# A spectral filter and feed-forward kernel: mirrored filter rows gathered in 7 of 16 blocks, after another piece of the input

## The chip, the cores and the metric

The kernel runs on one core of one Trainium2 chip. The metric is device time in microseconds (us) of one execution. A core has five engines that run at once, each through its own queue of instructions in order: TensorE (PE: matmuls, with its weight loads shown as PEld), VectorE (DVE), ScalarE (ACT), GpSimd (POOL) and SyncE (SP, which here only issues transfers). Transfers (DMA) are issued from the queues of SP, ACT and POOL and run beside the engines. An engine waits for another, or for a transfer, on a semaphore.

## The reference

One input x of 2048 rows and 448 columns goes through two kinds of layer, each twice. The first is a filter in the frequency domain, the second a feed-forward block with a squared relu; each is fed by a layer norm and added to x.

```python
def _A_ref(x, w_r, w_i):                     # x: [1, 2048, 448], w: [2048, 225]
    X = jnp.fft.rfft2(x.astype(jnp.float32), axes=(-2, -1))
    X = X * (w_r + 1j * w_i)
    return jnp.fft.irfft2(X, s=(S, D), axes=(-2, -1)).astype(jnp.bfloat16)

def _B_ref(x, w1, b1, w2, b2):               # 448 -> 1792 -> 448
    h = jnp.einsum("bsd,df->bsf", x, w1) + b1
    r = jnp.where(h > 0, h, 0)
    return jnp.einsum("bsf,fd->bsd", r * r, w2) + b2

x = A_x
x = x + _A_ref(_layernorm(x), A_w_r, A_w_i)
x = x + _B_ref(_layernorm(x), B_w1, B_b1, B_w2, B_b2)
x = x + _A_ref(_layernorm(x), A_w_r, A_w_i)
x = x + _B_ref(_layernorm(x), B_w1, B_b1, B_w2, B_b2)
```

All data are bfloat16, sums are float32.

## The kernel before

The 2048 rows are 16 row tiles of 128 (row 16p + t of x is partition p of tile t). All of x stays on the chip. The transforms are matmuls with constant matrices, in stages:

- *Norm and first transform* (tags A1, `ln_stats`, `first_A`). For each tile VectorE takes mean and variance (BN_STATS, BN_AGGR, lines 790 and 791), or ACT does with two passes over the tile (line 778); ACT takes a square root (line 654), VectorE the reciprocal (line 797). The transform matrix FA, scaled by that reciprocal, is Fs (line 672, GpSimd or VectorE); minus twice the mean is m (line 802). TensorE multiplies the tile with Fs, and ACT brings the sums from PSUM to XA (line 660). `GROUPS1` says which tiles are normed together and which of them on ACT (second number 1).
- *First filter* (`spectral(True)`): a transform along the columns (TD), one along the rows (B), the products with W (`stage_W`, tag W0) and the way back (Bi). The frequencies of the rows are in pairs p = 0 to 7. B's results for a pair are two halves, E and F. The products run on VectorE alone (TENSOR_TENSOR, line 687), first for pair 1, then 2 and 3, 4 and 5, 6 and 7, and last 0; each result Z is what Bi's matmuls wait for.
- *Feed-forward* (TI, AI, ln, h, o), a second norm and first transform (A2), the second filter (TD1 to Bi1) and the second feed-forward block.

W has to be there in rows as they come and in mirrored rows, since a pair uses a frequency and its mirror. `Wt` holds four slots for each pair 1 to 7: w_r, mirrored w_i, w_i, mirrored w_r. The two straight ones are plain loads on SP's queue. For the mirrored ones the kernel gathers: an iota makes a list of partitions in reverse (`back`, line 733), two gathers on GpSimd's queue (line 703) read w_i and then w_r by that list into `Wm`, which lies in the memory of yT, and 14 GpSimd copies (line 661, tags M.0 to M.6) take from each gathered row of 16 blocks of 225 the block that a pair needs, its columns 1 to 224. Pair p needs block 16 - p; the copies are blocks 15 down to 9.

The gathers are tied to one more thing than their list: the last argument of `gather` is a piece of x, `xin[:, 8, :]`, so that they start only when the piece with tile 8 has arrived.

The order of work on each engine is not that of the code. Every piece of work is a unit with a tag, and the table `ORDER` gives each unit a rank; `schedule` sorts by rank, hands out PSUM banks, and puts small filler matmuls (line 1302) where its own clock says that TensorE would be idle. A letter behind a rank puts the unit on ACT (a), VectorE (d) or GpSimd (p).

## Time and profile before

| | us |
|---|---|
| median of 3 runs | 276.46 |
| lowest and highest of them | 275.58, 277.64 |
| the profiled execution's own time | 275.05 |
| its span, from first to last instruction | 273.3 |
| busy in it: TensorE, VectorE, ACT, GpSimd | 259.6, 217.0, 169.5, 15.1 |

The profile is one execution. A line of its timeline has the start and length in us, the engine, the line of the kernel, the operation, what it writes and reads with their shapes, how many alike were merged, and in brackets how long the engine was idle before and what ended that. `<-issue` means that no wait shows. TensorE is busy for 95% of the span. The chain that ended last is followed back from the last instruction: at each step to what released it, or to the instruction before it on its engine.

### The profile page before, as it was taken

The page shows a single profiled execution, that of the slowest core. Times are in us where ns is not written, and L with a number is a line of the kernel's source. Part 1 is how long each engine was busy: PE and PEld are TensorE (multiplying, and loading weights), DVE is VectorE, ACT ScalarE, POOL GpSimd, SP SyncE. Part 2 cuts the span into 40 slices and gives each one's busy share as a digit, 9 for nine tenths or more (in the row PEclk, how much of TensorE's full clock was granted, in tenths as well). Part 3 has the DMA queues.
Part 4 walks back from the last instruction along what each step waited for, and adds up shares of the span by engine and source line. Part 5 has one row for each costly group of instructions (what it writes and reads, how often), then busy time and mean ns, then how long its engine had stood idle before and what let it go on. Part 6 is the DMA issues. An engine that isn't in the chain of part 4 may idle for free.

```text
span 273.3 us, 5853 instructions
## 1 busy us (share of the span) xinstructions
PE 259.6 (95%) x2198; PEld 158.6 (58%) x2198; DVE 217.0 (79%) x678; ACT 169.5 (62%) x387; POOL 15.1 (6%) x41
## 2 busy tenths in 40 slices
PE   8599749999999999999999999999999999999996
PEld 2477425779754554455557875779754454454554
DVE  5764899699999888697999999799697776345932
ACT  5796728698624982788314898597815834888000
POOL 2550800000000000000000000000000000000000
PEclk9999989999999999999999999999999999999999
DMA  6999590002220233100000000002130024200114
GB/s 192 375 323 305 172 306 23 0 2 40 41 44 25 43 52 59 38 2 0 2 1 0 5 2 0 0 5 41 38 70 6 0 58 93 57 2 0 36 46 139
DMA packets 27584, 18.06 MB, mean 66 GB/s; under 512 B 20226, under 2 KB 26082, under 8 KB 27428
## 3 DMA queue, kind: packets, MB, share of 16 engines
q1 hardware_dynamic: 26548, 14.87, 20.4%
q0 software_dynamic: 288, 1.84, 2.3%
q10 hardware_dynamic: 720, 0.98, 1.1%
q8 instruction: 17, 0.28, 0.5%
q14 instruction: 11, 0.09, 0.1%
HBM read 12.18 MB, written 1.84 MB: 51 GB/s over the span
## 4 chain that ended last, share of the span: by engine, by line
PE 81%; DVE 9%; DMA 6%; issue 1%; POOL 1%; ACTq 0%; ACT 0%; DVEq 0%
PE ps L635 81%; DVE tmp L687 5%; DMA yT<-in_A_w_r_dram,back 4%; DMA xin<-in_A_x_dram 2%; DVE x_sb L1078 2%; DVE arena L687 1%; DVE tmp L661 1%; DVE st L790 0%; POOL Fs L672 0%; ACTq L627 0%; DVE Fs L672 0%; ACT L727 0%; DVE x_sb L687 0%; POOL Wt L661 0%; DVE x_sb L1198 0%
## 5 line engine op out<-in xcount | busy, mean ns | idle before, releaser
L635 PE MATMUL ps<-yT,W_sb 64*128 64x512 bf16 (+1 forms) x770 | 89.8, 346 | 0.0
L635 PE MATMUL ps<-W_sb,arena 128*128 128x448 bf16 (+2 forms) x490 | 87.3, 336 | 0.0
L635 PEld LDWEIGHTS ps<-yT,W_sb 64*128 64x128 bf16 (+1 forms) x770 | 51.1, 95 | 36.4 <-issue 1.3
L635 PEld LDWEIGHTS ps<-W_sb,arena 128*128 128x128 bf16 x490 | 46.2, 98 | 36.7 <-DVE arena L1128 0.4
L654 ACT ACTIVATE arena<-ps,b1col 128x512 bf16<-128x512 f32 x84 | 51.8, 691 | 19.1 <-PE ps L635 19.0
L687 DVE TENSOR_TENSOR arena<-arena 128x512 bf16<-128x512 bf16 (+1 forms) x140 | 44.8, 363 | 17.0 <-ACT arena L654 16.9
L660 ACT ACTIVATE arena<-ps 128x448 bf16<-128x448 f32 (+1 forms) x41 | 24.3, 698 | 11.3 <-PE ps L635 11.1
L1102 ACT ACTIVATE VT<-x_sb 128x448 bf16<-128x448 bf16 x32 | 18.4, 577 | 19.9 <-DVE x_sb L1078 19.9
L1198 DVE SCALAR_TENSOR_TENSOR x_sb<-ps,arena 128x448 bf16<-128x448 f32 (+2 forms) x27 | 15.1, 564 | 9.6 <-PE ps L635 9.5
L654 ACT ACTIVATE mv<-mv,epst 128x1 f32<-128x1 f32 (+1 forms) x45 | 12.5, 297 | 13.0 <-DVE mv L791 6.8
L660 ACT ACTIVATE XA<-ps 128x512 bf16<-128x512 f32 x32 | 17.1, 593 | 4.7 <-PE ps L635 4.7
L654 ACT ACTIVATE arena<-ps 128x256 bf16<-128x256 f32 x56 | 17.1, 393 | 3.3 <-PE ps L635 3.2
L660 ACT ACTIVATE VT<-ps 128x512 bf16<-128x512 f32 (+1 forms) x27 | 13.9, 618 | 4.9 <-PE ps L635 4.9
L687 DVE TENSOR_TENSOR tmp<-arena,Wt 128x896 bf16<-128x896 bf16 (+1 forms) x24 | 12.3, 554 | 4.7 <-POOL Wt L661 4.6
L635 PE MATMUL ps<-yT,VT 64*128 64x512 bf16 x42 | 15.8, 376 | 0.0
L635 PE MATMUL ps<-arena,G_sb 128*128 128x448 bf16 (+1 forms) x76 | 15.3, 347 | 0.1
L635 PE MATMUL ps<-HS_sb,arena 128*128 128x512 bf16 x64 | 14.7, 379 | 0.1
L635 PE MATMUL ps<-H_sb,arena 128*128 128x256 bf16 x64 | 9.4, 292 | 5.5 <-DVE arena L687 5.4
L635 PE MATMUL ps<-TD_sb,XA 112*64 112x112 bf16 (+2 forms) x312 | 13.1, 224 | 0.0
L635 PEld LDWEIGHTS ps<-TD_sb,XA 112*64 112x64 bf16 (+2 forms) x312 | 12.1, 108 | 1.2 <-ACT arena L660 0.4
L635 PE MATMUL ps<-Fs,xin 128*128 128x256 bf16 x64 | 9.1, 272 | 3.5 <-POOL back L733 3.4
L635 PEld LDWEIGHTS ps<-H_sb,arena 128*128 128x128 bf16 x64 | 6.5, 105 | 8.6 <-DVE arena L687 6.5
(75 smaller groups left out, 304.2 us busy)
## 6 DMA issues: line engine op xcount, KB each, us to landing
out_dram<-x_sb SPq DMA_DIRECT2D x15, 112.0 KB, 1.8
W_sb<-in_B_w_dram SPq DMA_DIRECT2D x1, 1568.0 KB, 11.6
W_sb<-in_B_w_dram SPq DMA_DIRECT2D x1, 1344.0 KB, 6.3
HS_sb<-c_HS SPq DMA_DIRECT2D x1, 1024.0 KB, 11.4
G_sb<-c_G SPq DMA_DIRECT2D x1, 960.0 KB, 9.5
xin<-in_A_x_dram SPq DMA_DIRECT2D x1, 448.0 KB, 6.1
xin<-in_A_x_dram ACTq DMA_DIRECT2D x1, 448.0 KB, 6.9
Wt<-in_A_w_i_dram SPq DMA_DIRECT2D x1, 392.0 KB, 7.9
```

What stands on the lines that cost most here:

```text
L635: return sch.add("pe", lambda e: e.matmul(_res(o), lhsT, rhs, start=start, stop=stop, skip_group_check=skip), [lhsT, rhs], [o], cost=cost, ...
L654: sch.add("act", lambda e: e.activation(o, _res(i), func, **kw), rd, [o], cost=c)
L660: op = sch.add(engs[0], lambda e: e.activation(o, _res(i), ACT.Copy) if h[0].eng == "act" else e.tensor_copy(o, _res(i)), [i], [o], cost=c ...
L661: e.tensor_copy(o, _res(i)), [i], [o], cost=c[engs[0]], unit=unit)
L687: sch.add(eng, lambda e: e.tensor_tensor(o, _res(a), b, op), [a, b], [o], cost=_free(o) / rate + 69.0)
L1078: small(lambda e, xx=xx, xi=xi, r=r, m=m: e.scalar_tensor_tensor(out=xx, in0=_res(r), scalar=m, in1=xi, op0=ALU.subtract, op1=ALU.add), [r ...
L1102: sch.add("act", lambda e, i=i, o=o, x=x: e.activation(o, x, ACT.Square, accum_out=mv[:, i, 4:5]), [x], [o, mv[:, i, 4:5]], cost=560.0)
L1198: small(lambda e: e.scalar_tensor_tensor(out=o, in0=_res(i), scalar=r[0] if r else 1.0, in1=xb[:, t, d0:d1], op0=ALU.mult, op1=ALU.add), [ ...
```

## The change

Four things in the code, and a new `ORDER`:

1. The gathers read only the 7 blocks 9 to 15 that the copies use. The list `back` now holds the number of the first element, (16 (127 - p) + 9) x 225, W is seen as a column of single elements, and each partition gets 7 x 225 = 1575 elements where it got 3600.
2. The gathers are tied to `xin[:, 4, :]`, so to the piece of x with tiles 4 to 7.
3. That piece is one transfer on ACT's queue. Before, tiles 4 and 5 were ACT's and 6 and 7 SP's; tile 3 moves to SP's queue, and so does FA.
4. ACT takes the statistics of tiles 1, 4 and 6 instead of 1, 3 and 5, and tiles 6 and 7 are groups of their own.

The planner's clock also counts a transfer from GpSimd's queue as landed 7 us after its issue at the earliest.

```diff
-GROUPS1 = (((0,), 0), ((1,), 1), ((2,), 0), ((3,), 1), ((4,), 0), ((5,), 1), ((6, 7), 0), ((8, 9), 0), ((10, 11), 0), ((12, 13), 0),
-           ((14, 15), 0))
+GROUPS1 = (((0,), 0), ((1,), 1), ((2,), 0), ((3,), 0), ((4,), 1), ((5,), 0), ((6,), 1), ((7,), 0), ((8, 9), 0), ((10, 11), 0),
+           ((12, 13), 0), ((14, 15), 0))
...
-    "dve.warm": "1", "dve.epst": "0", "sp.xin": "6 11 16 18", "act.xin": "10 14 15 17", "act.FA_sb": "12",
+    "dve.warm": "4", "dve.epst": "0", "sp.xin": "5 12 18 21", "sp.FA_sb": "6", "act.xin": "11 17 20",
...
                     done[op] = dma_free = max(dma_free, t + 1800.0) + op.lat
+                    if e == "pool":
+                        done[op] = max(dma_free, t + 7000.0)
...
-        Wm = yT[:].rearrange("p a b c -> p (a b c)")[:, 0:2 * 16 * 225].rearrange("p (r k) -> p r k", r=2)
+        Wm = yT[:].rearrange("p a b c -> p (a b c)")[:, 0:2 * 7 * 225].rearrange("p (r k) -> p r k", r=2)
...
-        for n, (a, b, e) in enumerate(((0, 1, "sp"), (1, 2, "act"), (2, 3, "sp"), (3, 4, "act"), (4, 6, "act"), (6, 8, "sp"),
-                                       (8, 12, "act"), (12, 16, "sp"))):
+        for n, (a, b, e) in enumerate(((0, 1, "sp"), (1, 2, "act"), (2, 3, "sp"), (4, 8, "act"), (3, 4, "sp"), (8, 12, "act"),
+                                       (12, 16, "sp"))):
             dma(e, xin[:, a:b, :], x_dram[:, a:b, :])
-            if n == 2:
-                dma("act", FA_sb[:], dc["FA"])
+            if n == 0:
+                dma("sp", FA_sb[:], dc["FA"])
+            if n == 3:
                 sch.add("act", lambda e: e.activation(warm[:, 0:1], warm[:, 0:1], ACT.Sqrt), [warm[:, 0:1]], [warm[:, 0:1]],
...
-        sch.add("pool", lambda e: e.iota(back[:, 0:1], pattern=[[0, 1]], base=P - 1, channel_multiplier=-1), [],
+        sch.add("pool", lambda e: e.iota(back[:, 0:1], pattern=[[0, 1]], base=(16 * (P - 1) + 9) * 225, channel_multiplier=-16 * 225), [],
                 [back[:, 0:1]], cost=150.0)
...
-            gather(Wm[:, i, :], w.rearrange("(p k) l -> p (k l)", k=16), back[:, 0:1], xin[:, 8, :])
+            gather(Wm[:, i, :], w.rearrange("s (l o) -> (s l) o", o=1), back[:, 0:1], xin[:, 4, :])
...
-                evac(Wp[:, p, 3 - 2 * i, :], Wm[:, i, :].rearrange("p (k l) -> p k l", k=16)[:, 15 - p, 1:225], ["pool"])
+                evac(Wp[:, p, 3 - 2 * i, :], Wm[:, i, :].rearrange("p (k l) -> p k l", k=7)[:, 6 - p, 1:225], ["pool"])
```

The new `ORDER` moves instructions on every engine; the matmuls that compute something are the same in number. Three places are shown as the built programs have them, where lines of the changed kernel are two or three higher (672 is 674, 703 is 705, 802 is 805).

On GpSimd, from the first gather to the copies, before (m and Fs as above, `yT` is the memory of `Wm`, a number behind x counts what stands in a row):

```order
L703 DMA yT<-in_A_w_i_dram,back 128x3600
L672 TENSOR_SCALAR Fs<-FA_sb,rstd 128x256
L802 TENSOR_SCALAR m<-mv 128x1
L802 TENSOR_SCALAR m<-mv 128x2
L672 TENSOR_SCALAR Fs<-FA_sb,rstd 128x256
L802 TENSOR_SCALAR m<-mv 128x1
L672 TENSOR_SCALAR Fs<-FA_sb,rstd 128x256
L802 TENSOR_SCALAR m<-mv 128x2
L672 TENSOR_SCALAR Fs<-FA_sb,rstd 128x256 x3
L802 TENSOR_SCALAR m<-mv 128x2
L672 TENSOR_SCALAR Fs<-FA_sb,rstd 128x256
L703 DMA yT<-in_A_w_r_dram,back 128x3600
```

The same stretch in the changed kernel:

```order
L805 TENSOR_SCALAR m<-mv 128x1 x2
L705 DMA yT<-in_A_w_i_dram,back 128x1575
L805 TENSOR_SCALAR m<-mv 128x1
L674 TENSOR_SCALAR Fs<-FA_sb,rstd 128x256 x3
L805 TENSOR_SCALAR m<-mv 128x1 x2
L674 TENSOR_SCALAR Fs<-FA_sb,rstd 128x256
L805 TENSOR_SCALAR m<-mv 128x1 x2
L674 TENSOR_SCALAR Fs<-FA_sb,rstd 128x256 x2
L705 DMA yT<-in_A_w_r_dram,back 128x1575
L674 TENSOR_SCALAR Fs<-FA_sb,rstd 128x256 x2
L805 TENSOR_SCALAR m<-mv 128x2
L674 TENSOR_SCALAR Fs<-FA_sb,rstd 128x256 x3
```

Before, three Fs stand ahead of the first gather and seven between the two, with none behind, so that 10 precede the second; now no Fs precedes the first gather, six the second, and five follow it. In both the 14 copies come next.

On ACT, the statistics at the start, before (`yT` is scrap here, the waits are named by semaphore, `s_act_dma2` is the piece with tile 3 and `s_act_dma3` that with tiles 4 and 5):

```order
L778 ACTIVATE yT,mv<-xin 128x448 [waits s_act_dma0]
L654 ACTIVATE mv<-mv,epst 128x1 [waits s_dve]
L778 ACTIVATE yT,mv<-xin 128x448 [waits s_act]
L654 ACTIVATE mv<-mv,epst 128x1 [waits s_dve]
L778 ACTIVATE yT,mv<-xin 128x448 [waits s_act,s_act_dma2]
L654 ACTIVATE mv<-mv,epst 128x1 [waits s_dve]
L778 ACTIVATE yT,mv<-xin 128x448 [waits s_act]
L778 ACTIVATE yT,mv<-xin 128x448 [waits s_act,s_act_dma3]
L654 ACTIVATE mv<-mv,epst 128x1 [waits s_dve] x2
L654 ACTIVATE mv<-mv,epst 128x2 [waits s_dve]
L778 ACTIVATE yT,mv<-xin 128x448 [waits s_act]
L660 ACTIVATE XA<-ps 128x4x16x8 [waits s_pe] x2
```

In the changed kernel (`s_act_dma1` is the piece with tiles 4 to 7):

```order
L781 ACTIVATE yT,mv<-xin 128x448 [waits s_act,s_act_dma1]
L656 ACTIVATE mv<-mv,epst 128x1 [waits s_dve]
L781 ACTIVATE yT,mv<-xin 128x448 [waits s_act]
L656 ACTIVATE mv<-mv,epst 128x1 [waits s_dve] x2
L781 ACTIVATE yT,mv<-xin 128x448 [waits s_act]
L656 ACTIVATE mv<-mv,epst 128x1 [waits s_dve]
L781 ACTIVATE yT,mv<-xin 128x448 [waits s_act]
L656 ACTIVATE mv<-mv,epst 128x1 [waits s_dve]
L662 ACTIVATE XA<-ps 128x4x16x8 [waits s_pe]
```

Two of six passes stood behind the piece with tiles 4 and 5; now four stand behind the piece with tiles 4 to 7, with five roots among them, ahead of the first evacuation to XA.

On VectorE, where the first stage ends and the products begin, before:

```order
L672 TENSOR_SCALAR Fs<-FA_sb,rstd 128x256
L661 CAST arena<-ps 128x448 [waits s_pe] x5
L687 TENSOR_TENSOR tmp<-arena,Wt 128x448 [waits s_pool,s_sp_dma7,s_dve]
L687 TENSOR_TENSOR tmp<-arena,Wt 128x448 [waits s_pool,s_sp_dma4]
L687 TENSOR_TENSOR tmp<-arena,Wt 128x448 [waits s_act]
L687 TENSOR_TENSOR tmp<-arena,Wt 128x448
L687 TENSOR_TENSOR tmp<-tmp 128x448 [waits s_dve] x2
```

In the changed kernel:

```order
L674 TENSOR_SCALAR Fs<-FA_sb,rstd 128x256 [waits s_pe,s_dve]
L663 CAST arena<-ps 128x448 [waits s_pe] x2
L663 CAST arena<-ps 128x448
L663 CAST arena<-ps 128x448 [waits s_pe]
L689 TENSOR_TENSOR tmp<-arena,Wt 128x448 [waits s_pool,s_sp_dma5,s_dve]
L689 TENSOR_TENSOR tmp<-arena,Wt 128x448 [waits s_pool,s_sp_dma8]
L689 TENSOR_TENSOR tmp<-arena,Wt 128x448 [waits s_act]
L689 TENSOR_TENSOR tmp<-arena,Wt 128x448
L689 TENSOR_TENSOR tmp<-tmp 128x448 [waits s_dve] x2
```

One cast left VectorE (ACT has it); each of the first two products waits for one copy of GpSimd, the third for ACT, in both.

190 rows, old and new, of the table ORDER are left out of this document.

## The prediction

> **What bounds the kernel now.** I read the page's share of engines first, then who TensorE waited for, then the chain that ended last in order of time, then each queue in the stretch that the chain pointed to.
>
> ```profile
> span 273.3 us, 5853 instructions
> PE 81%; DVE 9%; DMA 6%; issue 1%; POOL 1%; ACTq 0%; ACT 0%; DVEq 0%
> ```
> TensorE carries 81% of the chain, so only what is not TensorE on that chain can be won without taking matmuls away. In order of time (start, length, what):
>
> ```profile
> 1.15 0.47 ACTq L627
> ...
> 2.13 6.24 DMA xin<-in_A_x_dram
> ...
> 9.81 1.80 PE ps L635 x15
> ...
> 17.20 10.94 DMA yT<-in_A_w_r_dram,back
> ...
> 28.19 0.38 POOL Wt L661
> ...
> 28.66 2.35 DVE tmp L687 x5
> ...
> 47.12 5.30 PE ps L635 x32
> ...
> 57.70 116.99 PE ps L635 x1090
> ```
> From 57.7 us on it is TensorE almost without a break. Before that stand two things that are not: the load of x up to 8.4 us, and, from 17.2 to 47.1 us, one gather (10.94 us), a GpSimd copy that waits for it, and a row of VectorE products. The windows (stretch, its length, then busy time of PE, PEld, DVE, ACT, POOL; clock; DMA) say which engine that second stretch hangs on:
>
> ```profile
> 32.00:36.00 4.00, 1.81 (x12) 1.09 (x12) 4.00 (x8) 1.64 (x2) 2.09 (x4) 1.00 0.96 338
> 36.00:40.00 4.00, 1.78 (x8) 0.89 (x9) 4.00 (x11) 0.00 (x0) 0.00 (x0) 0.86 0.99 302
> 40.00:44.00 4.00, 4.00 (x25) 2.85 (x24) 4.00 (x9) 2.29 (x4) 0.00 (x0) 0.71 0.37 116
> PE ps L635 <- DVE arena L687: 5.4, 2, 3.9
> ```
> VectorE is full, TensorE is under half busy up to 40 us and waits 5.4 us for it. TensorE's granted clock falls to 0.86 and 0.71 after that waiting; since VectorE sets the pace there, I count nothing for it. VectorE's own timeline, first filter stage (the products with W):
>
> ```profile
> 23.01 0.62 DVE L661 CAST arena<-ps 128x448 bf16<-128x448 f32 x1 [0.46 <-PE ps L635]
> 23.67 0.39 DVE L687 TENSOR_TENSOR tmp<-arena,Wt 128x448 bf16<-128x448 bf16 x1
> 28.66 1.40 DVE L687 TENSOR_TENSOR tmp<-arena,Wt 128x448 bf16<-128x448 bf16 x3 [4.60 <-POOL Wt L661]
> ...
> 32.37 1.49 DVE L687 TENSOR_TENSOR tmp<-arena 128x896 bf16<-128x896 bf16 x2
> 33.78 2.39 DVE L687 TENSOR_TENSOR tmp<-tmp,Wt 128x896 bf16<-128x896 bf16 x4
> ...
> 38.38 1.14 DVE L687 TENSOR_TENSOR tmp<-arena 128x896 bf16<-128x896 bf16 x2
> 39.45 2.22 DVE L687 TENSOR_TENSOR tmp<-tmp,Wt 128x896 bf16<-128x896 bf16 x4
> ...
> 48.55 0.39 DVE L687 TENSOR_TENSOR arena<-tmp 128x448 bf16<-128x448 bf16 x1
> ```
> One product, 4.60 us of nothing, then no pause to 48.9 us. So this is a chain on VectorE of 20.3 us, started late by a gather. GpSimd's timeline says why the gather is late:
>
> ```profile
> 9.19 0.48 POOL L672 TENSOR_SCALAR Fs<-FA_sb,rstd 128x256 bf16<-128x256 bf16 x1 [3.43 <-DVE rstd L797]
> ...
> 10.61 1.16 POOL L703 DMA_INDIRECT yT<-in_A_w_i_dram,back  x1 [0.25 <-PE ps L635]
> ...
> 16.57 0.48 POOL L672 TENSOR_SCALAR Fs<-FA_sb,rstd 128x256 bf16<-128x256 bf16 x1 [0.61 <-DVE rstd L797]
> 17.20 1.01 POOL L703 DMA_INDIRECT yT<-in_A_w_r_dram,back  x1 [0.16 <-issue]
> 18.86 0.37 POOL L661 COPY Wt<-yT 128x224 bf16<-128x224 bf16 x1 [0.65 <-DMA yT<-in_A_w_i_dram,back]
> 28.19 5.90 POOL L661 COPY Wt<-yT 128x224 bf16<-128x224 bf16 x13 [8.96 <-DMA yT<-in_A_w_r_dram,back]
> ```
> The second gather stands last behind all scaled matrices Fs. The first took 8.2 us to land (10.61 to 18.8), the second 10.9.
>
> **The change, part by part.**
>
> *When the gathers run.* Both now read 7 of 16 blocks, 44% of the bytes. The w_i gather waits for row tiles 4 to 7, call their arrival T, and the w_r gather stands behind six Fs of GpSimd instead of ten. Arrivals, from the DMA list (KB, us from issue to landing), with the mean rate of the first 30 us:
>
> ```profile
> DMA packets 6981, 8.39 MB, mean 280 GB/s; under 512 B 4625, under 2 KB 5889, under 8 KB 6850
> ...
> H_sb<-c_H SPq DMA_DIRECT2D x1, 384.0 KB, 12.8
> ...
> xin<-in_A_x_dram ACTq DMA_DIRECT2D x1, 224.0 KB, 6.2
> ```
> Tiles 4 and 5 arrived at 8.4 us (2.13 + 6.24) with 512 KB of ACT's queue moved. Tiles 4 to 7 end 560 KB of it and are ACT's second transfer, not its fourth, so issued at 1.15. By the same 6.24 us T is 7.4, by bytes 8.4 x 560/512 = 9.2; I take 7.8, nearer the first, as one long row per partition replaces short ones. The w_i gather is then issued at 7.9; behind it GpSimd does six Fs at 0.48, small ones, and two waits for TensorE, some 4.8 us, so w_r is issued at about 12.7 instead of 17.2. For the landing: between 3.6 us (8.2 scaled by 44%) and 10.9 (the bytes do not matter); I take 6, nearer the first, since the gathers moved against a full load. So w_r lands near 18.7, between 16.3 and 23.6. GpSimd is through with its own Fs at about 18, and 14 copies of 0.37 then end at about 24, where they ended at 34.1.
>
> *What VectorE wins.* Its order there keeps its form, casts and then the products, with nothing between that the wait would hide. (a) The wait of 4.60 us goes: the first copy needed is made before 23.7. (b) The copies leave the stretch of the products, and those run faster without them. The same ten operations in the second filter stage, where GpSimd does nothing:
>
> ```profile
> 156.70 1.29 DVE L687 TENSOR_TENSOR tmp<-arena,Wt 128x448 bf16<-128x448 bf16 x4
> ...
> 159.08 1.15 DVE L687 TENSOR_TENSOR tmp<-arena,Wt 128x896 bf16<-128x896 bf16 x2
> 160.15 0.26 DVE L687 TENSOR_TENSOR arena<-tmp 128x224 bf16<-128x224 bf16 x1
> ```
> They need 156.70 to 159.08 and a last 0.26, 2.6 us; in the first stage 0.39 and 28.66 to 32.37, 4.1 us. Then 1.49 against 1.14 and 2.39 against 2.22. Together 1.5 + 0.35 + 0.17 = 2.0 us. I take 1.6, since a few copies may still overlap the first products; bounds 0 and 2.0. The Trainium skill, SBUF — State Buffer, "Who interferes with whom", says a VectorE instruction with two SBUF inputs and a GpSimd instruction that reads SBUF block each other fully. By that the 13 copies would hold up to 13 x 0.37 = 4.8 us, and the forecast would be some 3 us lower. The rows show 2.0 at most, so I keep the rows. (c) New: the first two products need the half that VectorE itself casts, the third the half that ACT casts; I charge 0.2.
>
> *The first stage (norm, Fs, first transform).* ACT is its densest engine:
>
> ```profile
> 8.40 0.58 ACT L778 ACTIVATE yT<-xin 128x448 bf16<-128x448 bf16 x1 [0.38 <-DMA xin<-in_A_x_dram]
> ...
> 10.42 0.52 ACT L654 ACTIVATE mv<-mv,epst 128x1 f32<-128x1 f32 x2 [0.34 <-DVE mv L781]
> ...
> 11.40 1.06 ACT L660 ACTIVATE XA<-ps 128x512 bf16<-128x512 f32 x2
> ...
> 17.45 3.10 ACT L660 ACTIVATE XA<-ps 128x512 bf16<-128x512 f32 x6
> ...
> 26.81 3.97 ACT L660 ACTIVATE arena<-ps 128x448 bf16<-128x448 f32 x8 [0.18 <-PE ps L635]
> ```
> ACT still takes the statistics of three tiles, but of tiles 4 and 6 only after T: four passes of 0.58 and five roots of 0.26 are 3.7 us, so its evacuations start at 11.5 instead of 11.4; 16 of them and five roots took 9.15 us to 20.55. The stage ends 0.2 us later; with T's ends, 0.3 earlier to 1.5 later. GpSimd's gather of 1.16 us now stands ahead of the Fs of tile 2, yet VectorE needs 1.4 us after T for that tile's reciprocal, which covers it. If T were early and the statistics quick, the gather would cost up to its 1.16. FA moves from ACT's to SP's queue, and VectorE makes the first Fs, so tile 0 is multiplied before T; that is small and falls into time in which TensorE waits anyway. The iota moves to the front of an idle GpSimd, and the copies read the same 224 columns as before: nothing for either.
>
> *SP's queue.* TD goes ahead of G, W2 ahead of W1, J to the end. The last load wanted early is H's 384 KB:
>
> ```profile
> 16.41 0.59 SPq L627 DMA_DIRECT2D H_sb<-c_H  x1
> ```
> It landed at 16.41 + 12.8 = 29.2 us, the last of some 7.8 MB on all queues; now 6.6 MB stand up to its end, so at 280 KB/us it lands about 4 us earlier, at 25, and it is wanted after 27. I charge nothing; uncovered, it would cost what it is late.
>
> *What is late next.* With the chain 6 us earlier, ACT must supply it: up to the fourth product group it makes 16 more evacuations alone from about 26.4, near the row of 26.81: ten at 0.50, four of double width charged as two each, two of 512 columns at 0.52 (3.10 over 6), 10.0 us, so 36.4. VectorE began that group at 42.7 (39.45 + 2.22 and 1.1 of sums) and would ask at about 36.8. Covered by 0.4 us. I charge 0.3, bounds 0 and 2.5.
>
> *The rest.* ORDER is new for the whole program, with the same matmuls from 58 us on apart from fillers. TensorE is dense there, so I charge 0, bounds -0.5 and +1.5.
>
> Sum: -4.6 - 1.6 + 0.2 + 0.2 + 0.3 = -5.5 us against the profiled execution, 275.05 us (span 273.3 and 1.75 around it), so 269.5. The median of the three runs shown, 276.46, is 1.4 higher: **271.0 us**.
>
> **Rivals.**
>
> *The gathers land late.* For: the second took longer than the first with the same bytes, so queueing counts more than size. If w_r takes 10.9 us again, it lands at 23.6: 0.3 us of wait, and the copies stay beside the products (0 for (b)). -4.6 + 0.3 + 0.2 + 0.2 + 0.2 = -3.7, so 272.8. The Trainium skill, SBUF — State Buffer, section "SBUF: two separate sides", gives a reason: VectorE in a two-port mode keeps GpSimd from writing descriptors; its example goes from 0.62 to 3.1 us. By that the landing near 18.7 would be some 21.2, and the time between the two. Against it: issued in a full VectorE stretch, the first gather took 1.16 us to issue, the other 1.01.
>
> *The first stage is late.* If T is 9.2, it ends 1.5 later instead of 0.2, so 272.3; this is the end of T by bytes. For it: one large piece is awaited where two tiles sufficed. Against it: it is issued two places earlier.
>
> *The gain is given back.* ACT's cover fails (2.5) and the new order loses 0.7 elsewhere: -2.5, so 274.0; the row for it is ACT's 26.81, dense.
>
> *Slower: the gathers fall to pieces.* The new gather indexes a view whose rows have one element. If each row were fetched in many pieces instead of one of 3150 bytes, the list's 6981 packets of 30 us over 16 engines give 69 ns a packet and engine; at 1575 pieces a row, 201,600 for a gather, it takes 870 us. With w_r at 28.1 as before nothing would be won; over 1% is lost once it lands after 28.1 + 2.8 = 30.9, 18.2 us after its issue, and that takes 18.2 / 0.069 x 16 / 128 = 33 pieces a row. Against it: the order shows one transfer of 128x1575, the form of the old one. Time: anywhere over 279.
>
> **How the numbers follow.** As forecast 0.52 (269.0 to 272.2), late gathers 0.14, late first stage 0.11, given back 0.18, pieces 0.05. The range reaches down for a full 2.0 in (b), the early T and the runs' own 1 us below their median, and up through the first two rivals and half the third: 268.5 to 274.2. One per cent, 2.8 us, is about what a measurement can tell from no change. Faster (under 273.7) takes 0.52, 0.13, 0.09 and 0.04 of these cases, 0.78; slower is the last, 0.05; the rest, 0.17, lies within.
>
> **What would show it.** Right: VectorE's products start at about 24 us without a wait for POOL; copies over by about 25; the 128x224 sums 0.2 to 0.3 us and not 0.43; the last Bi matmul near 46; 57.7 becomes about 52. Wrong: w_r landing after 22, XA evacuations ending after 21.5, VectorE waiting for ACT between 26 and 43, or TensorE pauses after 58 that were not there.

## The result, and the profile of the changed kernel

The changed kernel takes 267.26 us in the median of four runs (267.04 to 270.39), the kernel before 276.2 in four (one more than in the table above); the ratio is 0.9695 with a 95% interval of 0.9614 to 0.9777. It is faster, as forecast, but by 3.7 us more than the 271.0 of the forecast, and it lies 1.2 us below the range. The profiled execution took 267.06 us, with a span of 265.3 us; before it was 275.05 and 273.3.

The page of the changed kernel, its span and the shares of the chain that ended last:

```profile
span 265.3 us, 5857 instructions
PE 85%; DVE 11%; DMA 1%; issue 1%; SPq 0%; ACT 0%; DVEq 0%
```

The share of DMA on the chain fell from 6% to 1%: the gather is off it. What the gathers and copies do now, in GpSimd's timeline (start, length, line, what; in brackets the idle time before and what ended it):

```profile
7.21 1.16 POOL L705 DMA_INDIRECT yT<-in_A_w_i_dram,back  x1 [0.44 <-POOL m L805]
...
12.33 1.02 POOL L705 DMA_INDIRECT yT<-in_A_w_r_dram,back  x1 [0.16 <-issue]
...
17.02 0.36 POOL L663 COPY Wt<-yT 128x224 bf16<-128x224 bf16 x1
18.79 4.48 POOL L663 COPY Wt<-yT 128x224 bf16<-128x224 bf16 x13 [1.40 <-DMA yT<-in_A_w_r_dram,back]
```

The w_r gather is issued at 12.3 us (17.2 before), lands at 18.8 (28.1 before), and the copies are over at 23.3 (34.1 before). VectorE's timeline from tile 2's statistics to the end of the products:

```profile
5.42 0.63 DVE L793 BATCH_NORM_STATS2 st<-xin 128x6 f32<-128x448 bf16 x1 [1.27 <-DMA xin<-in_A_x_dram]
...
20.16 1.77 DVE L663 CAST arena<-ps 128x448 bf16<-128x448 f32 x3 [0.95 <-PE ps L637]
21.96 1.85 DVE L689 TENSOR_TENSOR tmp<-arena,Wt 128x448 bf16<-128x448 bf16 x4
...
24.33 0.82 DVE L689 TENSOR_TENSOR arena<-tmp 128x224 bf16<-128x224 bf16 x4
25.08 1.15 DVE L689 TENSOR_TENSOR tmp<-arena 128x896 bf16<-128x896 bf16 x2
26.15 2.22 DVE L689 TENSOR_TENSOR tmp<-tmp,Wt 128x896 bf16<-128x896 bf16 x4
...
40.74 0.39 DVE L689 TENSOR_TENSOR arena<-tmp 128x448 bf16<-128x448 bf16 x1
```

Three things are to be read there against the rows of before. The products start at 21.96 us and not at 23.67. No wait for POOL stands in the chain; it was 4.60 us. And the chain without that wait takes 41.13 - 21.96 = 19.17 us instead of 48.94 - 23.67 - 4.60 = 20.67. Together 1.71 + 4.60 + 1.50 = 7.81 of the 8.0 us; from the end of the products on the two kernels run alike to 0.2 us. TensorE in the stretch in which it waited 5.4 us for VectorE before:

```profile
PE ps L637 <- DVE arena L689: 0.6, 1, 0.6
```

Where the first 1.71 us come from is seen on ACT, whose densest stretch is the first stage (norm, scaled matrices Fs, first transform):

```profile
6.30 0.29 ACT L656 ACTIVATE mv<-mv,epst 128x1 f32<-128x1 f32 x1 [1.26 <-DVE rstd L800]
6.50 0.56 ACT L781 ACTIVATE yT<-xin 128x448 bf16<-128x448 bf16 x1
...
10.13 0.57 ACT L662 ACTIVATE XA<-ps 128x512 bf16<-128x512 f32 x1
...
16.12 3.01 ACT L662 ACTIVATE XA<-ps 128x512 bf16<-128x512 f32 x6
```

Tile 4's statistics start at 6.50 us without a wait for the load: tiles 4 to 7 were there already, and what held ACT was the root of tile 2, whose load ended at 5.42. The evacuations start at 10.13 (11.40 before), the last six at 16.12 (17.45 before), and they end at 19.13 (20.55 before): 1.4 of the 1.71 us. The other 0.3 were not traced.

### The profile page after: what moved, and what is told of

Read it like the earlier page. It is cut to its first block, busy times and chain, and to the rows that moved or that the text cites. A ratio compares the mean times of both kernels' runs of the same rounds, so it can differ in the third digit from the quotient of the medians.

```text
span 265.3 us, 5857 instructions
## 1 busy us (share of the span) xinstructions
PE 258.1 (97%) x2198; PEld 157.9 (60%) x2198; DVE 211.8 (80%) x672; ACT 173.0 (65%) x396; POOL 14.1 (5%) x41
## 4 chain that ended last, share of the span: by engine, by line
PE 85%; DVE 11%; DMA 1%; issue 1%; SPq 0%; ACT 0%; DVEq 0%
PE ps L637 84%; DVE tmp L689 4%; DVE x_sb L1081 2%; DMA xin<-in_A_x_dram 1%; DVE arena L689 1%; DVE st L793 1%; DVE tmp L663 1%; DVE arena L663 1%; DVE yT L663 0%; DVE mv L784 0%; PE ps L1305 0%; SPq L629 0%; ACT mv L656 0%; DVE mv L794 0%; DVE rstd L800 0%
## 5 line engine op out<-in xcount | busy, mean ns | idle before, releaser
L662 ACT ACTIVATE arena<-ps 128x448 bf16<-128x448 f32 (+1 forms) x43 | 24.9, 677 | 2.0 <-PE ps L637 1.9
L1201 DVE SCALAR_TENSOR_TENSOR x_sb<-ps,arena 128x448 bf16<-128x448 f32 (+2 forms) x27 | 15.0, 567 | 12.6 <-PE ps L637 12.5
L656 ACT ACTIVATE arena<-ps 128x256 bf16<-128x256 f32 x56 | 18.3, 392 | 2.7 <-PE ps L637 2.5
L656 ACT ACTIVATE mv<-mv,epst 128x1 f32<-128x1 f32 (+1 forms) x46 | 13.2, 296 | 9.0 <-DVE mv L794 6.8
L637 PE MATMUL ps<-arena,G_sb 128*128 128x448 bf16 (+1 forms) x76 | 14.4, 333 | 0.1
L637 PE MATMUL ps<-TD_sb,XA 112*64 112x112 bf16 (+2 forms) x312 | 13.7, 224 | 0.0
L689 DVE TENSOR_TENSOR tmp<-arena,Wt 128x896 bf16<-128x896 bf16 (+1 forms) x24 | 12.3, 563 | 0.1
L1081 DVE SCALAR_TENSOR_TENSOR x_sb<-ps,mv,xin 128x448 bf16<-128x448 f32 x16 | 10.4, 677 | 0.8 <-PE ps L637 0.8
L662 ACT ACTIVATE tmp<-ps 128x896 bf16<-128x896 f32 (+1 forms) x13 | 10.1, 806 | 1.4 <-PE ps L637 1.4
```

Of the source, the lines that this page charges most:

```text
L637: return sch.add("pe", lambda e: e.matmul(_res(o), lhsT, rhs, start=start, stop=stop, skip_group_check=skip), [lhsT, rhs], [o], cost=cost, ...
L656: sch.add("act", lambda e: e.activation(o, _res(i), func, **kw), rd, [o], cost=c)
L662: op = sch.add(engs[0], lambda e: e.activation(o, _res(i), ACT.Copy) if h[0].eng == "act" else e.tensor_copy(o, _res(i)), [i], [o], cost=c ...
L689: sch.add(eng, lambda e: e.tensor_tensor(o, _res(a), b, op), [a, b], [o], cost=_free(o) / rate + 69.0)
L1081: small(lambda e, xx=xx, xi=xi, r=r, m=m: e.scalar_tensor_tensor(out=xx, in0=_res(r), scalar=m, in1=xi, op0=ALU.subtract, op1=ALU.add), [r ...
L1201: small(lambda e: e.scalar_tensor_tensor(out=o, in0=_res(i), scalar=r[0] if r else 1.0, in1=xb[:, t, d0:d1], op0=ALU.mult, op1=ALU.add), [ ...
```

## The experiments

Theory at this point: the gain is the wait for the gather (4.6 us), the copies out of the products (1.5) and a first stage that ends earlier because x lands earlier (1.7). Rivals: the smaller gathers relieve all loads; or the new order of statistics brings the first stage.

### The gathers: bytes and place

All 16 blocks again, in the new place (the gather, the iota and the copies' index go back to their old form, `xin[:, 4, :]` stays):

```diff
-Wm = ...[:, 0:2 * 7 * 225]...
+Wm = ...[:, 0:2 * 16 * 225]...
...
-gather(Wm[:, i, :], w.rearrange("s (l o) -> (s l) o", o=1), back[:, 0:1], xin[:, 4, :])
+gather(Wm[:, i, :], w.rearrange("(p k) l -> p (k l)", k=16), back[:, 0:1], xin[:, 4, :])
...
```

> The changed kernel, but both gathers read all 16 blocks again (922 KB each instead of 403 KB). Theory (the bytes matter because they set when w_r lands): w_i is issued at about 7.2 us and w_r at about 12.3 as in the changed kernel, w_r takes about 10.9 us as before the change and lands at about 23.2; VectorE's first product group waits about 1.3 us for it, the copies lie beside the products again and stretch them by about 1.5 us: 267.3 + 2.8 = 270 us. Rival one (only the place in the queue matters): no change, 267.3. Rival two (the bytes slow every load of the first 20 us): the first stage ends later too, over 272.

268.86 us (268.12 to 269.34). The first stage did not move (products at 21.96 again), so the bytes do not slow the loads of x. GpSimd's timeline in its profile (268.12 us):

```profile
20.70 5.20 POOL L663 COPY Wt<-yT 128x224 bf16<-128x224 bf16 x13 [3.31 <-DMA yT<-in_A_w_r_dram,back]
```

VectorE in the same profile:

```profile
24.87 1.33 DVE L689 TENSOR_TENSOR arena<-tmp 128x224 bf16<-128x224 bf16 x4
26.13 1.15 DVE L689 TENSOR_TENSOR tmp<-arena 128x896 bf16<-128x896 bf16 x2
```

The landing is 1.9 us later, still ahead of the products: no wait. The copies reach 2.6 us further into the products, and the first group ends at 26.13 instead of 25.08: 1.05 us, the whole difference of the two spans (266.3 and 265.3); the medians differ by 1.6. I had 1.3 us of wait too many.

Only the bytes, in the kernel before (its iota, `Wm` and the copies' index change as in the section on the change):

```diff
-gather(Wm[:, i, :], w.rearrange("(p k) l -> p (k l)", k=16), back[:, 0:1], xin[:, 8, :])
+gather(Wm[:, i, :], w.rearrange("s (l o) -> (s l) o", o=1), back[:, 0:1], xin[:, 8, :])
...
```

> The kernel before, with one thing changed: the gathers read 7 of 16 blocks. Order, pieces of x and the wait for tile 8 stay. Theory: w_r is still issued at about 17.2 us, but lands in 6.4 to 7 us, at about 23.9; VectorE's wait of 4.6 us goes almost wholly, the copies stay beside the products and cost their 1.5 us: 276.2 - 4.3 = 271.9 us. Rival (the place in the queue and not the bytes sets the landing): w_r takes 10.9 us again, 276.2 us. If copies beside products cost nothing, it would be 270.4 or less.

274.41 us (273.56 to 276.21), ratio 0.9927 (0.9891 to 0.9963): 1.8 us and not 4.3. In its profile (273.71 us) w_r took 8.3 us from issue to landing, where I had 6.4 to 7 from the changed kernel; issued late (18.98 us), the small gather is not that quick. TensorE ran at half clock there until 16 us, so the products start at 25.81; the wait that is left is 1.60 us.

The place alone undone: w_r behind all eleven Fs in the changed kernel (its rank is the first of the two numbers).

```diff
-"pool.yT": "107 65"
+"pool.yT": "138 65"
```

> The changed kernel, with the w_r gather moved back behind all scaled matrices of GpSimd. Theory: it is issued at about 17.1 instead of 12.3 us; with 403 KB it lands 6.4 to 8.3 us later, at 23.5 to 25.4, so VectorE's first products wait 1.5 to 3.4 us for the copies, and the copies lie beside the products and stretch them by 1.5 us less the 0.5 that they cost already: 267.3 + 2.5 to 4.4, taken 270.8 us. Rival (the smaller gather is so quick that its place does not matter): 267.3.

273.72 us (273.35 to 274.35), ratio 0.9896 (0.9870 to 0.9922). GpSimd's timeline in its profile:

```profile
17.72 1.02 POOL L705 DMA_INDIRECT yT<-in_A_w_r_dram,back  x1 [0.16 <-issue]
...
26.19 5.90 POOL L663 COPY Wt<-yT 128x224 bf16<-128x224 bf16 x13 [7.06 <-DMA yT<-in_A_w_r_dram,back]
```

VectorE's in the same:

```profile
22.45 0.39 DVE L689 TENSOR_TENSOR tmp<-arena,Wt 128x448 bf16<-128x448 bf16 x1
26.66 1.40 DVE L689 TENSOR_TENSOR tmp<-arena,Wt 128x448 bf16<-128x448 bf16 x3 [3.82 <-POOL Wt L663]
27.98 1.02 DVE L689 TENSOR_TENSOR tmp<-tmp 128x448 bf16<-128x448 bf16 x2
28.93 1.51 DVE L689 TENSOR_TENSOR arena<-tmp 128x224 bf16<-128x224 bf16 x4
```

The picture of before is back: one product, a wait, and products at the slower rate. 8.4 us to land, 3.82 of wait, and the first group takes 30.36 - 22.45 - 3.82 = 4.1 us instead of 3.1. The place is worth most of the gain, the bytes about a fifth; each is taken alone, and they do not add up, since a gather that lands early enough hides its bytes. What the tie to tiles 4 to 7 instead of tile 8 brings by itself was not tried.

w_r directly behind w_i, to have the copies out of the products altogether:

```diff
-"pool.yT": "107 65"
+"pool.yT": "66 65"
```

> The changed kernel, with the w_r gather directly behind the w_i gather on GpSimd. It is issued at about 8.5 instead of 12.3 us and lands by about 16; the copies then end by about 22.5 instead of 23.3 and leave most of the first product group, which takes 2.6 instead of 3.1 us. Against it: the scaled matrices of tiles 4 and on are made 1.0 us later, and TensorE already waited 0.27 us for one of them. Theory (the first stage is paced by GpSimd's scaled matrices and ACT together): -0.5 + up to 1.0, 266.8 to 267.8. Rival (there is slack in the first stage, so only the copies count): 266.8. Rival (the gathers against x's last loads make them late): over 268.3.

268.78 us (267.88 to 270.19), ratio 0.9699 (0.9666 to 0.9732), no better than the changed kernel. In the profile, of the longest run, the copies were over at 25.1, ahead of the products, and the first group took 2.6 us as expected; but TensorE ran the first transform at half speed until 13.6 us, and ACT waited 2.94 us for it. That I had not expected, and it led to the runs on the clock below.

### The copies beside the products

Fourteen more copies on GpSimd into a part of yT that nothing reads; nobody waits for them.

```diff
...
+for p in range(14):
+    sch.tag = "X"
+    evac(scr[:, p % 2, :], Wm[:, p % 2, 225 * (p // 2) + 1:225 * (p // 2) + 225], ["pool"])
```

> The changed kernel, with 14 more copies of the same size on GpSimd behind the 14 it makes, into a part of yT that nothing reads; they lie beside VectorE's products from about 23.3 to 29 us and nobody waits for them. Theory (a GpSimd copy slows the VectorE instruction beside it, by the sum of the rows of before: 2.0 us over 13 copies, 0.15 each): 1.5 to 2 us longer, taken 269.0 us; sums of 128x224 at 0.43 instead of 0.27, products of 128x896 by two tenths longer. Rival one (no interference, what was slow before was something else): 267.3. Rival two, from a page, the Trainium skill, SBUF - State Buffer, section Who interferes with whom: VectorE with two SBUF inputs and GpSimd block each other fully; then 14 x 0.37 = 5.2 us, 272.5.

270.86 us (269.61 to 271.40), ratio 0.9770 (0.9738 to 0.9803). GpSimd's timeline in its profile:

```profile
23.25 6.79 POOL L664 COPY yT<-yT 128x224 bf16<-128x224 bf16 x14
```

and VectorE's:

```profile
23.30 1.99 DVE L690 TENSOR_TENSOR tmp<-arena,Wt 128x448 bf16<-128x448 bf16 x4
...
26.16 1.51 DVE L690 TENSOR_TENSOR arena<-tmp 128x224 bf16<-128x224 bf16 x4
27.60 1.50 DVE L690 TENSOR_TENSOR tmp<-arena 128x896 bf16<-128x896 bf16 x2
29.02 2.56 DVE L690 TENSOR_TENSOR tmp<-tmp,Wt 128x896 bf16<-128x896 bf16 x4
```

Each row is as slow as its partner in the kernel before or slower (1.51, 1.49 and 2.39 there). The chain of products took 21.05 us against 19.17 (from 23.30 to 44.35), 1.9 us for 14 copies, 0.13 each; and the copies themselves 0.49 instead of 0.32 (4.18 over the 13 ahead of them). Both slow down, neither stands still: the full block of 5.2 us did not come. The products also began 1.3 us later than in the changed kernel, with TensorE at half clock again until 10.7 us, and 1.1 us lie behind them, where TensorE's clock reads 0.73 and 0.84 from 36 to 44 us; so the time is above the 269.0 that I gave, while the part under test came out.

### How x is loaded

The changed kernel with x and FA in the pieces and on the queues of before:

```diff
-((0, 1, "sp"), (1, 2, "act"), (2, 3, "sp"), (4, 8, "act"), (3, 4, "sp"), (8, 12, "act"), (12, 16, "sp"))
+((0, 1, "sp"), (1, 2, "act"), (2, 3, "sp"), (3, 4, "act"), (4, 6, "act"), (6, 8, "sp"), (8, 12, "act"), (12, 16, "sp"))
...
-dma("sp", FA_sb[:], dc["FA"])
+dma("act", FA_sb[:], dc["FA"])
...
```

> The changed kernel, but x and FA come in the pieces, on the queues and in the order of before. Theory (the first stage ends 1.75 us earlier because tiles 4 to 7 arrive about 2 us earlier): ACT's statistics of tile 4 start at about 8.4 instead of 6.5, its last evacuations of the first transform end at about 20.9 instead of 19.1, VectorE's products start at about 23.7 instead of 21.96, and the time is about 267.3 + 1.75 = 269.0 us. Rival (the new order of statistics and scaled matrices brought it, the pieces nothing): 267.3, products at 22. What speaks against neither: gathers issued later by the same 2 us, w_r landing at about 21, still ahead of the products.

272.08 us (269.48 to 272.40), ratio 0.9845 (0.9792 to 0.9899). It held more than one cause: ACT issued tiles 3 to 5 behind its table load, later than before the change, and the profile (269.48 us) is that of a run 2.6 us below its median. So it was mended: the same pieces, issued ahead of the table load (in `ORDER`, ranks 16 and 17 for them and 19 for the table load, where the run above had 18, 18 and 17).

> As the run with x in the pieces of before (272.1 us in the median, 269.5 in its profile), but ACT issues tiles 3 to 5 ahead of its table load; there they stood behind it and were issued about 1 us later than in the kernel before, so that the arrival of tiles 4 and 5 (9.34 us) was later than the 8.40 of before. Theory (the first stage follows the arrival of tiles 4 to 7): ACT's statistics of tile 4 start at 8.4, VectorE's products at 21.96 + 1.9 = 23.9, the copies end ahead of most of the products (W0.0 in 2.6 us instead of 3.1), time about 268.8 us. Rival one (the order, not the pieces): 267.3. Rival two (more and smaller pieces make the landing uncertain whatever the issue): runs spread over more than 2 us again, median over 270.5.

271.50 us (270.93 to 272.54), ratio 0.9811 (0.9776 to 0.9846); the runs lie within 1.6 us, so rival two's spread did not come, though its median did. ACT's timeline in its profile:

```profile
8.77 0.58 ACT L780 ACTIVATE yT<-xin 128x448 bf16<-128x448 bf16 x1 [3.13 <-DMA xin<-in_A_x_dram]
```

TensorE's:

```profile
11.67 1.01 PE L637 MATMUL ps<-Fs,xin 128*128 128x256 bf16 x4 [3.67 <-POOL Fs L674]
```

and TensorE's windows (stretch, its length, busy time, granted clock, share of the DMA engines, KB/us):

```profile
12.00:14.00 2.00, 2.00 (x12) 0.50 1.04 387
14.00:16.00 2.00, 2.00 (x11) 0.50 1.11 254
```

Tiles 4 and 5 land at 8.8 us. TensorE stands 3.67 us, its granted clock is then 0.50, and four matmuls of 256 columns take 1.01 us instead of 0.60. To take the two effects apart, eight matmuls on ones, which nothing reads, were put into that pause:

```diff
+EXTRA = {2: 8}
+for _ in range(EXTRA.get(npe, 0)):
+    ...
+    self.ops["pe"].append(d)
```

> The run with x in the pieces of before and ACT's issue mended (271.5 us; first transform at half clock, 1.01 us for four matmuls of 256 columns where the changed kernel has 0.60), with eight more of the matmuls on ones, whose results nothing reads, ahead of TensorE's second real group, in its pause of 3.7 us. Theory (the pieces cost it twice: tiles 4 to 7 land 2 us later, and the longer pause halves TensorE's clock): the clock stays, 0.60 us for four, and 2 to 2.7 us of the 4.2 go: 268.8 to 269.5. Rival one (the clock halves by chance, whatever TensorE does): 271.5 as before. Rival two (the late arrival alone costs it): 271.5.

269.17 us (268.99 to 272.02), ratio 0.9732 (0.9652 to 0.9811). ACT's timeline in its profile (269.35 us):

```profile
9.22 0.58 ACT L793 ACTIVATE yT<-xin 128x448 bf16<-128x448 bf16 x1 [3.61 <-DMA xin<-in_A_x_dram]
```

TensorE's:

```profile
12.12 0.60 PE L650 MATMUL ps<-Fs,xin 128*128 128x256 bf16 x4 [2.64 <-POOL Fs L687]
```

and VectorE's:

```profile
24.75 1.37 DVE L702 TENSOR_TENSOR tmp<-arena,Wt 128x448 bf16<-128x448 bf16 x4
26.03 0.69 DVE L702 TENSOR_TENSOR tmp<-tmp 128x448 bf16<-128x448 bf16 x2
26.64 0.82 DVE L702 TENSOR_TENSOR arena<-tmp 128x224 bf16<-128x224 bf16 x4
```

The clock stays up although the load is later still, and 2.2 us come back by the two ratios. Their intervals overlap: one of the four runs, 272.02 us, stayed with those of the run above, and it has no profile. Against the changed kernel on the same chip (267.49) the pieces and FA's queue alone cost 1.7 us with the clock held. Under the new order, but in the old pieces, the products start at 24.75 us, later than the 23.67 of before. So how x is loaded, and not the order of the statistics, makes the first stage early.

Which part of them? FA back on ACT's queue, tiles 4 to 7 left in one piece:

```diff
-dma("sp", FA_sb[:], dc["FA"])
+dma("act", FA_sb[:], dc["FA"])
...
```

> The changed kernel, with FA back as the second transfer of ACT's queue; tiles 4 to 7 stay in one piece, now ACT's third. Theory one (tiles 4 to 7 land early because their transfer is started early, at 1.15 us): issued about 0.45 us later, landed 0.5 us later, 267.3 to 267.8. Theory two (FA's 512-byte rows ahead of x on the same queue cause the dip to 130 to 200 KB/us at 3 to 4.5 us that all kernels with FA on ACT show): the dip comes back and tiles 4 to 7 land 1.5 to 2 us later, 269 us.

268.29 us (267.52 to 269.76), ratio 0.9693 (0.9634 to 0.9753). ACT's timeline in its profile (269.76 us):

```profile
8.44 0.58 ACT L781 ACTIVATE yT<-xin 128x448 bf16<-128x448 bf16 x1 [3.17 <-DMA xin<-in_A_x_dram]
```

the rates of its DMA in 40 slices of the first 30 us:

```profile
GB/s 0 0 60 328 196 99 222 321 360 372 388 360 327 310 327 341 399 464 416 378 189 117 117 208 365 296 382 360 359 387 322 297 349 371 332 343 344 338 338 348
```

and the same row of the changed kernel:

```profile
GB/s 0 0 48 286 334 363 363 337 382 376 330 313 316 332 409 418 442 392 369 169 173 196 286 197 432 371 356 355 327 283 355 361 346 339 339 342 342 330 271 184
```

The dip stands in the fifth to seventh slices, 3.0 to 5.2 us: 196, 99, 222 against 334, 363, 363; before the change it was 204, 131, 255. All 17 profiles of before, the changed kernel and the runs sort by it: the sixth slice reads 99 to 197 in the seven with FA on ACT's queue and 241 to 366 in the ten with FA on SP's. Tiles 4 to 7 land at 8.4 us in one piece too. So theory two: a transfer of 64 KB ahead of x on that queue, and not the size of the pieces, is what made the load late. (The run also takes FA off SP's queue, whose later transfers start up to 0.5 us earlier; that part was not separated.) The time is another matter: the median is about 1 us longer, the ratio is not told apart from that of the changed kernel. Of the 2 us of the landing some 0.5 come back, since the copies are over before products that start later (first group 2.6 us). Its profile is of its longest run, with TensorE at a clock of 0.55 from 12 to 14 us.

The other half, tiles 4 to 7 in two pieces with FA on SP:

```diff
-(2, 3, "sp"), (4, 8, "act"), (3, 4, "sp"),
+(2, 3, "sp"), (4, 6, "act"), (6, 8, "act"), (3, 4, "sp"),
...
```

> The changed kernel, with tiles 4 to 7 in two pieces of 224 KB, one after the other as ACT's second and third transfers, where it has one of 448 KB. Theory one (started early is what counts): tiles 4 and 5 land no later, 267.3 us. Theory two (one long row per partition is what makes it fast, 3584 bytes instead of 1792): the pieces land 1 us or more later, with a dip of the rate, 268.5 us or more.

269.46 us (268.05 to 271.03), in two pairs: 268.05 and 268.24, 270.69 and 271.03. The median is that of theory two, but not for its reason. In the profile of 270.69 us tile 4 waited for no load, as theory one has it, and the pieces took 3.8 us. What was late was tile 2 on SP's queue, 6.11 instead of 5.42 us; TensorE stood 2.12 us for tile 0 behind it and then ran at half speed:

```profile
7.55 1.01 PE L637 MATMUL ps<-Fs,xin 128*128 128x256 bf16 x4 [2.12 <-DVE mv L784]
```

Whether the split made tile 2 late is open.

And the new pieces, with FA on SP's queue, in the kernel before, with all else as it was there:

> The kernel before, with one thing changed: x and FA come in the pieces, on the queues and in the order of the changed kernel. Theory: tiles 4 to 7 are there at about 6.3 us instead of 8.4, the first stage ends 1.75 us earlier, and with it the last scaled matrix and the issue of the w_r gather (about 15.5 instead of 17.2); this lands at about 26.4 if it takes 10.9 again, so the whole moves by about 1.75 us: 274.5. Rival one (the pieces bring nothing, the order of the statistics does): 276.2. Rival two (the gather's landing is set by the load and not by its issue, it stays at 28.1): 276.2 too, but with the first stage earlier and a longer wait of VectorE, about 6.3 us.

275.29 us (274.21 to 277.46), ratio 0.9966 (0.9938 to 0.9994): 0.9 us (0.2 to 1.7 by the interval) and not surely the 1.7 of the theory. Its profile is that of its longest run, with tile 2 landing at 8.25 us and TensorE at half clock, so it does not show the step; what the pieces bring there alone stays open.

### TensorE's clock

The changed kernel once more, beside the next runs:

> The changed kernel, unchanged, on the chip of the three runs beside it. Theory (a run whose TensorE keeps its full clock through the first transform takes 267 us, one whose clock halves after the idle time at 5.4 us takes about 3 us more): most runs at 266.9 to 267.6, one in four or so near 270.4, nothing between. Rival (the runs vary by the arrival of loads): spread evenly over 2 us or more.

267.49 us (267.13 to 268.04): no run near 270. In its profile (267.40) TensorE's first four matmuls take 0.60 us, as in the first profile of the changed kernel. The one run of 270.39 stays unexplained, since it has no profile.

Without the matmuls on ones ahead of 9 us:

```diff
-if not (cold or recent < self.warm_share * self.WINDOW):
+if f < 9000.0 or not (cold or recent < self.warm_share * self.WINDOW):
```

> The changed kernel without the 17 or so matmuls on ones ahead of 9 us, whose results nothing reads. Theory: TensorE comes to the first transform at half clock in every run, four matmuls of 256 columns take 1.0 us instead of 0.60 until about 3.4 us of dense work have passed; ACT waits for TensorE, and the first stage ends 2 to 3 us later: 269.5 to 270.5. Rival (ACT's 19 evacuations and roots are the bound of the first stage, TensorE has slack at half clock too): 267.3.

268.16 us (268.00 to 268.74). TensorE's timeline in its profile:

```profile
7.08 1.01 PE L637 MATMUL ps<-Fs,xin 128*128 128x256 bf16 x4 [7.08 <-DVE mv L784]
...
11.54 0.94 PE L637 MATMUL ps<-Fs,xin 128*128 128x256 bf16 x4
...
12.49 0.60 PE L637 MATMUL ps<-Fs,xin 128*128 128x256 bf16 x4
```

and VectorE's:

```profile
23.39 1.37 DVE L689 TENSOR_TENSOR tmp<-arena,Wt 128x448 bf16<-128x448 bf16 x4
```

Half speed until about 12 us, as expected; but it costs 0.7 us and not 2 to 3. The products start 0.9 us after those of the run above (22.49), and 0.3 come back because the copies are over by then. How long half clock holds does not set its cost alone: 0.7 us here, to about 12 us, and 2.2 in the run with the mended pieces, to about 17; but in the profiles of the split pieces and of w_r behind w_i, where it holds to about 13.5, the products start 2.9 and 3.6 us later than in the changed kernel.

Tile 2's statistics behind tile 0's work on VectorE, so that the 1.27 us of wait at 5.42 holds up nothing:

```diff
-"A1.2": "13 15 34 38 16p 67p 70 71"
+"A1.2": "34 34 34 38 35p 67p 70 71"
```

> The changed kernel, with VectorE's statistics of row tile 2 moved behind the reciprocal and the scaled matrix of tile 0, and GpSimd's m2 of tile 2 after them. There VectorE stood 1.27 us waiting for tile 2 to land (5.42 us) with tile 0's work behind it, and TensorE stood 1.43 us for tile 0 (until 6.86). Theory: tile 0 is multiplied at about 5.4, TensorE has no pause there, the clock never halves, and tile 1's root comes before 5.7, so the first stage ends 0 to 0.4 us earlier: 266.8 to 267.3 us in every run. Rival (tiles 4 to 7 pace it, and the pause was harmless): 267.3 with an odd run at 270.

267.28 us (267.03 to 267.38) beside 267.49 (267.13 to 268.04): no difference that can be measured, though its four runs lie within 0.35 us. TensorE's pause is gone (the four matmuls stand at 5.24 and take 1.04 us), the next one is longer (1.11 us instead of 0.27), and the products start at 22.08.

Last, the kernel before with twelve matmuls on ones in its pause of 3.36 us (as above, with `EXTRA = {1: 12}`):

> The kernel before, with 12 more matmuls on ones, whose results nothing reads, in TensorE's pause of 3.36 us ahead of its first real group (6.45 to 9.81 us). Theory (in some of its runs the clock halves in that pause; the profiled run of 275.05 us was one in which it did not): every run has 0.60 us for four matmuls of 256 columns, the runs above 276.5 go, median 275.0 to 275.6 instead of 276.2 to 276.9. Rival (before's spread comes from the landing of its gathers): median and spread unchanged.

275.33 us (274.33 to 276.96), ratio 0.9967 (0.9937 to 0.9997). The median is the one expected, but one run is still above 276.5, and the spread (2.6 us) is not gone. So the clock in that pause is a part of what lies between the profile of before (275.05) and its median, and not the whole.

A second stretch of low clock is left, behind TensorE's wait for VectorE's products. TensorE's windows in this run's profile (276.19 us):

```profile
36.00:40.00 4.00, 1.58 (x6) 0.65 1.02 330
40.00:44.00 4.00, 4.00 (x19) 0.50 0.23 72
```

The profile of before has 0.86 and 0.71 there, the changed kernel

```profile
36.00:40.00 4.00, 3.88 (x19) 1.00 0.03 7
40.00:44.00 4.00, 4.00 (x28) 1.00 0.00 0
```

From the end of the last product to the end of the span this run takes 225.2 us, the kernel before 224.4, and the kernel before with 7 blocks, whose clock is 1.00 there, 223.8. (The changed kernel takes 224.2.) The 46 runs of the kernel before beside these experiments fit: nine with a mean granted clock of 0.994 took 275.0 to 275.8 us, five with 0.975 took 278.3 to 278.8. That is an agreement and not a test; no run held the clock up in this stretch alone.

## Why the forecast was too high

The gather's mechanism was right; the first stage, the cover and the step to the median were not.

- *(a) the wait of 4.60 us goes.* Right, to the number: it is gone, and moving w_r back brought 3.82 of it back. The forecast landing of 18.7 us was measured as 18.79, the issue of w_r as 12.3 (12.7).
- *(b) 1.6 us for the copies.* Right: 1.50 by the two chains. Fourteen copies put back at will cost 1.9.
- *The first stage, +0.2.* Wrong, this is the step that failed: it ended 1.71 us earlier, a miss of 1.9. The arrival T of tiles 4 to 7 was taken as 7.8 us, between 7.4 and 9.2; ACT used them at 6.50 without waiting. Both ends came from one row of before, 6.24 us for the transfer of tiles 4 and 5. That transfer was itself slowed by FA ahead of it on the same queue, and the change moves FA away: with FA back, T is 8.44 in one piece. The prediction called FA's move "small"; it carried the arrival. How much of the time hangs on FA alone is not shown: with FA back the median is 1 us longer, the ratio is not told apart.
- *(c) the cast, +0.2, and ACT's cover, +0.3.* Nothing of either: VectorE's chain has no wait between 21.96 and 41.1 us. A miss of 0.5.
- *The rest, 0.* About -0.2 (8.0 less 7.81).
- *From the profiled run to the median, +1.4.* Wrong: it was 0.2 for the changed kernel, a miss of 1.2. The distance was that of one draw of before to its median. Fillers in before's pause take 0.8 us of its median away, so a part of that distance was TensorE's clock in a pause that the changed kernel does not have. Another part goes, as far as the profiles show, with the clock of 0.86 and 0.71 that the prediction read behind the wait for VectorE and counted as nothing: in the changed kernel it stays at 1.00 there, and in the run with w_r behind all Fs, where the wait is back, it reads 0.60 from 36 to 40 us. How the 1.2 us divide between the two stretches is not shown.

1.9 + 0.5 + 0.2 - 0.1 + 1.2 = 3.7 us. (The third rival's sum comes to -2.6 and 273.9, not -2.5 and 274.0; nothing hangs on it.) Of the rivals none came: the gathers landed on time (w_r 6.4 us after its issue), the first stage was early, nothing was given back, and the gathers moved in 160 packets with the rest of that queue (288 before). What was to be late next, H's load, took 7.9 us and held nobody up.

## What to carry to other kernels

A row that prices a transfer carries its neighbours' price in it: before scaling it to a new size, ask which of those neighbours the change moves, even if they are only 64 KB. For a gather that feeds the start of a chain, look first at its place in the issuing engine's order and then at its bytes: here the place was worth 6 us, the bytes 1 to 2. And the distance from a profiled run to the median belongs to the kernel that was measured; it is not carried over unless its cause is known.

## What the runs showed of the hardware that was not expected

- After a pause in its first real work TensorE can run at half speed for microseconds, and the length of the pause alone does not decide it. Four matmuls of 256 columns took 0.60 us after pauses of 1.43, 1.94, 2.64, 3.36 and 3.71 us (the changed kernel twice, the filled pieces, before, FA on ACT's queue, where the clock reads 0.55 from 12 us on all the same), and 0.97 to 1.01 after 0.61, 2.12, 2.29, 2.41, 2.96 and 3.67 (the pieces of before as first tried, split pieces, w_r behind w_i, more copies, 7 blocks in before, mended pieces). The Trainium skill, TensorE: Matmul & The Clock Gate, Part 1, says that the clock is halved after an idle window of some 3.4 us that runs free of the kernel. The 3.67 agrees, and a free-running window would explain why runs of one kernel differ; the 0.61 to 2.96 us do not follow from it, unless the clock had not come up yet in the first 5 us. The rows ahead of the pause tell for some: with the split pieces and with w_r behind w_i ten matmuls on ones of 512 columns took 4.45 us, and with the first pieces nine took 4.02, so 0.45 each, where seven later ones in the changed kernel took 1.57, 0.22 each. There the clock had not come up. With more copies (ten in 3.67) and 7 blocks in before (sixteen in 5.83) it had in part, and those two stay open. In the changed kernel the ten took 4.45 as well, and the clock came up during the pause. In the profiles of the split pieces and of w_r behind w_i the clock column read 1.00 while the matmuls took twice as long, so the durations are the surer sign.
- With the 64 KB of FA ahead of x on ACT's queue, instead of SP's, the rate of all queues dipped to 99 to 222 KB/us for 2 us and tiles 4 to 7 landed 2 us later. Why so small a transfer does so was not tried.
- The same w_r gather of 403 KB took from 4.6 us (the pieces of before, issued at 15.3) over 6.4 (the changed kernel, at 12.3) and 7.9 (right behind the other, at 9.5) to 8.4 (last, at 17.7). Size moved it by about as much: 922 KB issued at 12.5 took 8.2, and 10.9 at 17.2.
- A GpSimd copy of 128x224 beside VectorE's products of two SBUF inputs cost VectorE 0.13 us in the mean of 14, and went from 0.32 to 0.49 itself. The Trainium skill, SBUF — State Buffer, "Who interferes with whom", has a full block, 0.37 each by the rows of before; the measurement decides.
